# Two decode layers over a long KV cache: when a K slot is transposed, and who copies it back

## The chip, the cores and the metric

The kernel runs on one core of a Trainium2 chip. The metric is device time in microseconds, the median of several runs. A profile of one execution was taken beside it.

## The reference

Batch 8, one new token per row, model width 512, 32 query heads in 8 groups (one K/V head each, head size 128), a cache of 8192 positions, all in bf16. The same attention block, with the same weights and the same cache, and the same feed-forward block are applied twice:

```
x = A_x                                        # [8, 1, 512]
for layer in (0, 1):
    q = layernorm(x) @ wq                      # 32 heads of 128
    s = einsum(q, k_cache) * 128 ** -0.5       # k_cache [8, 8, 8192, 128]
    o = einsum(softmax(s), v_cache)            # v_cache [8, 8, 8192, 128]
    x = x + o @ wo
    x = x + silu(layernorm(x) @ w1) @ w2       # w1 [512, 1792]
```

## The kernel before

The work is cut into 128 **tasks**, one for each layer, batch row and K/V head. A task has 8 positions called **granules** (GPT = 8); a granule is 8 chunks of 128 cache rows. Two granules (GPG = 2) make a **slot**: 2048 cache rows of K or V, 512 KB, 4 KB in each of 128 partitions of an SBUF arena with NSLOT = 28 slots. So a task reads 4 slots of K and 4 of V.

Because both layers read the same cache, K of heads 3 to 7 (20 slots, KEEP) is kept in its transposed form from layer 0 to layer 1 of the same batch row. `make_tasks` orders the tasks so that it can be: after the first row come repeating groups of about 16, in which 5 layer-0 tasks with a home for their K ("home tasks") are followed by some 6 tasks of heads 0 to 2 of either layer ("streaming tasks", K and V pass through the remaining 8 slots), then by the 5 layer-1 tasks whose K lies in the arena ("kept tasks", only V is loaded). 88 tasks transpose their K, 40 don't.

One loop over positions p (from L830) emits everything; the order in which it emits is the order of each engine's queue. In a task with transposes:

- `emit_t` (L503) transposes one granule on TensorE, 8 matmuls against the identity into one of three PSUM banks TPp (L512), and copies the bank back over the raw K in the arena, on ScalarE (L518) or VectorE (L520). Three copies in eight, by the numbers in ACT_EVAC, go to ScalarE.
- `emit_t_until(p + LT)` keeps the transposes LT = 2 positions ahead of the score.
- At each odd p, `emit_s` (L537, matmuls L543) scores the slot that ends there: 4 matmuls over 512 columns each. Then `emit_pv` (L605, L616) multiplies two granules of V that lie LP = 12 positions back, 16 matmuls. I call these two positions a step.
- The softmax of the task just scored runs in pieces at set positions of the next task (the table `soft`, L817): row maximum at 0; the shift, by a small matmul (L564), and the exponential on ScalarE (L576) at 1; row sums at 3; the transposes of P (`emit_pt`, L592, in a TPp bank as well) at 4; the reciprocal at 7.
- The rest of a batch row's layer (output projection, layer norms, feed-forward, next query) is a list `chain`, of which one or two pieces are emitted per position. `add_heads` puts pieces of the output projection (L711) into kept and home tasks.

All loads go through SyncE's queue, in the order of `plan_loads` (L188). It takes the loads by their `need`, the position where they are first read, and gives each a slot by when that slot falls free (`free`), on an assumed clock of 1.24 us a position (0.64 where K is kept). A load is issued at the position `after`, when its slot's last reader is emitted; SyncE then waits for that reader. For K the need is LT positions ahead of the first granule:

```
need = -1 if i0 < PRE else i0 - LT
...
need = i0 + GPG - 1 + LP          # V
```

V loads are tried four slots wide, then two, then one: a wide one is taken only if its lead on the assumed clock is at least EARLIEST (14 us for four, 9 for two). Among free slots the planner takes the longest lead up to ENOUGH = 10 us, then the least waste, then the latest slot. Home K is loaded four slots at once, streaming K one slot at a time (KWIDE = 1).

Engines are ordered by semaphores: `op` makes an instruction wait for the last writer of what it reads and for all readers of what it overwrites. A score waits for both halves of its slot, and a copy for its transposes.

Of the kernel before, what the change touches and what calls it, by code (L numbers as in the profile page):

```python
# [14 lines left out]
GPT = 8  # L15
GPG = 2
NSLOT = 28
KEEP = 20
LT = 2
PRE = 10  # L20
KWIDE = 1
VWIDE = 4
# [1 line left out]
ENOUGH = 10.0  # L24
# [12 lines left out]
PVN = 12  # L37
CW = 32
SETTLE = 1
ACT_EVAC = (1, 4, 7)  # L40

BF16 = mybir.dt.bfloat16
FP32 = mybir.dt.float32
# [144 lines left out]
def plan_loads(tasks, kept, nslot, ngran):  # L188

    at = {t: i for i, t in enumerate(tasks)}  # L190
    homes = make_homes(kept, nslot, ngran)
    clock = [0.0]
    for layer, _b, g in tasks:
        for i in range(GPT):
            clock.append(clock[-1] + PACE[int(layer == 1 and (g, i // GPG) in kept)])
    clock += [clock[-1] + PACE[0] * (n + 1) for n in range(LP + GPT)]

    heap = []

    def push(kind, i, ks, home=None):  # L200
        layer, b, g = tasks[i]
        i0 = i * GPT + ks[0] * GPG
        if kind == "K":
            need = -1 if i0 < PRE else i0 - LT
            end = i if home is None else at[(1, b, g)]
            free = [end * GPT + (k + 1) * GPG - 1 for k in ks]
        else:
            need = i0 + GPG - 1 + LP
            free = [i * GPT + (k + 1) * GPG - 1 + LP for k in ks]
        heapq.heappush(heap, (need, kind, i, ks, Load(kind, i, b, g, ks, need, free, home)))  # L210

    def split(ks, width):
        return [ks[n:n + width] for n in range(0, len(ks), width)]

    reserved = [[] for _ in range(nslot)]
    for i, (layer, b, g) in enumerate(tasks):
        if layer == 0 and g in homes:
            ks, slot = homes[g]
            push("K", i, ks, slot)
            for n in range(len(ks)):  # L220
                reserved[slot + n].append(i * GPT + ks[0] * GPG - LT)
        for ks in split([k for k in range(ngran) if (g, k) not in kept], KWIDE):
            push("K", i, tuple(ks))
        for ks in split(list(range(ngran)), VWIDE):
            push("V", i, tuple(ks))

    def lead(need, after):
        return clock[max(0, need)] - clock[after] if after >= 0 else FAR

    free = [-2] * nslot  # L230
    loads = []
    while heap:
        d = heapq.heappop(heap)[-1]
        n = len(d.ks)
        if d.home is not None:
            for m in range(n):
                reserved[d.home + m].pop(0)
        else:
            best = None
            for slot in range(nslot - n + 1):  # L240
                held = free[slot:slot + n]
                if any(r and lead(r[0], f) < AHEAD for r, f in zip(reserved[slot:slot + n], d.free)):
                    continue
                after = max(held)
                waste = sum(clock[max(0, after)] - clock[max(0, f)] for f in held)
                key = (-min(lead(d.need, after), ENOUGH), waste, -after, slot)
                best = key if best is None else min(best, key)
            if n > 1 and (best is None or -best[0] < EARLIEST[n]):
                push(d.kind, d.task, d.ks[:n // 2])
                push(d.kind, d.task, d.ks[n // 2:])  # L250
                continue
            d.slot = best[-1]
        d.after = max(free[d.slot:d.slot + n])
        assert d.after < d.need or d.need == -1 and d.after == -2, (d.kind, d.need, d.after)
        free[d.slot:d.slot + n] = d.free
        loads.append(d)
    return loads

# [17 lines left out]
def _build(ctx, nc, A_x, A_k_cache, A_v_cache, A_wq, A_wo, B_w1, B_w2, out):  # L276
# [18 lines left out]
    NG = len(tasks) * GPT  # L295
# [20 lines left out]
    def chunk(slot, c):  # L316
        o = slot * SLOT + c * 128
        return ARENA[:, o:o + 128]
# [121 lines left out]
    with nc.Block() as block:  # L440

        @block.sync
        def _(sync_eng):
# [45 lines left out]
            load_rest()  # L489

            evacs = [0]
            tevacs = [0]
            tnext = [0]

            def has_t(i):
# [3 lines left out]
            def where(i):  # L499
                _l, b, g = tasks[i // GPT]  # L500
                return b, g, (i % GPT) // GPG, i % GPG

            def emit_t(i):  # L503
                b, g, k, h = where(i)
                slot = k_slot[(b, g, k)]
                n = tevacs[0]
                tevacs[0] += 1
                tb = evacs[0] % NTP
                evacs[0] += 1
                tpv = TPp[tb][:, :].rearrange("p (k q) -> p k q", q=128)  # L510
                steps = [
                    lambda c=c: pe.transpose(tpv[:, c, :], chunk(slot, h * GRP + c), ident[:, :])  # L512
                    for c in range(GRP)
                ]
                mm_group(steps, reads=[r_half(slot, h), "ident"], writes=[f"TP{tb}"])
                dst = half(slot, h)
                if n % 8 in ACT_EVAC:
                    op(act, lambda: act.copy(dst, TPp[tb][:, :]), reads=[f"TP{tb}"], writes=[r_half(slot, h)])  # L518
                else:
                    op(dve, lambda: dve.tensor_copy(dst, TPp[tb][:, :]), reads=[f"TP{tb}"], writes=[r_half(slot, h)])  # L520

            def emit_t_until(i):
                while tnext[0] <= min(i, NG - 1):
                    if has_t(tnext[0]):
                        emit_t(tnext[0])
                    tnext[0] += 1
# [10 lines left out]
            def emit_s(i):  # L537
                ti = i // GPT
                b, g, k, _h = where(i)
                slot = k_slot[(b, g, k)]  # L540
                bank, qn = ti % NSCP, ti % NQB
                steps = [
                    lambda c=c: pe.matmul(  # L543
                        SCp[bank][c * QUAD:(c + 1) * QUAD, :], QB[qn][:, NGRAN - 1 - k:NGRAN - 1 - k + QUAD],
                        ARENA[:, slot * SLOT + c * KB:slot * SLOT + (c + 1) * KB],
                        start=(k == 0), stop=(k == NGRAN - 1),
                    )
                    for c in range(NQ)
                ]
                mm_group(steps, reads=[r_half(slot, 0), r_half(slot, 1), f"QB{qn}"], writes=[f"SC{bank}"])  # L550
# [279 lines left out]
            for p in range(NG + LP + GPT + 1):  # L830
                tq = (p + LQ) // GPT
                if (p + LQ) % GPT == 0 and tq < ntask:
                    layer, b, _g = tasks[tq]
                    if layer == 1 and chain and chain_b[0] == b:
                        while chain:
                            chain.pop(0)()
                    emit_q(tq)
                emit_t_until(p + LT)
                if p % GPG == GPG - 1:
                    if p < NG:  # L840
                        emit_s(p)
                    for i in range(p - LP - GPG + 1, p - LP + 1):
                        if 0 <= i < NG:
                            emit_pv(i)
                ti, ph = p // GPT - 1, p % GPT
                if 0 <= ti < ntask and ph in soft:
                    for f in soft[ph]:
                        f(ti)
                if chain:
                    left = max(1, first1[chain_b[0]] - EARLY - p)  # L850
                    late = len(chain) <= QPARTS or len(chain) > left + QPARTS // 2
                    for _n in range(2 if late and len(chain) > left else 1):
                        chain.pop(0)()
                elif heads[turn[0]] and (p >= NG or turn[0] == B
                                         or p % GPG == GPG - 1 and (tasks[p // GPT][2], 0) in kept):
                    add_heads(turn[0])
                done = p - LP - GPT
                if done >= 0 and done % GPT == 0 and done // GPT < ntask:
                    tj = done // GPT
                    emit_norm(tj)  # L860
                    layer, b, _g = tasks[tj]
                    if layer == 0:
                        heads[b].append(_g)
                    elif b == B - 1:
                        heads[B].append(_g)
                    if layer == 0 and tj == last0[b]:
                        assert not chain and turn[0] == b
                        chain.extend([lambda b=b: add_heads(b)] * (HKV - summed[b]) + chain_of(b))
                        chain_b[0] = b
                        turn[0] = b + 1  # L870
                issue_until(p)
# [48 lines left out]
```

## Time and profile before

| | |
|---|---|
| median of 3 runs | 1208.91 us (1202.98 to 1213.16) |
| the profiled execution | 1205.91 us, span on the core 1204.2 us |
| busy: TensorE matmuls | 975.9 us (81%) |
| busy: VectorE | 597.2 us (50%) |
| busy: ScalarE | 374.0 us (31%) |
| bytes by DMA | 467.94 MB, mean 389 GB/s |
| mean granted TensorE clock | 0.957 |
| K loads | 192 of 512 KB, 40 of 2048 KB |
| V loads | 256 of 512 KB, 128 of 1024 KB |
| copies of transposed K | 440 on VectorE (0.690 us each), 264 on ScalarE (1.009 us each) |

Busy times are sums over an engine's instructions; a busy share says nothing by itself of what an engine waits for, and the DMA share is a mean over 16 DMA engines. PE is TensorE's matmuls, PEld its weight loads, which overlap them; a matmul's duration includes its way through the array, so the distance from start to start is what counts when the engine's pace is read.

### The profile page before, as it was taken

The page shows a single profiled execution, that of the slowest core. Times are in us where ns is not written, and L with a number is a line of the kernel's source. Part 1 is how long each engine was busy: PE and PEld are TensorE (multiplying, and loading weights), DVE is VectorE, ACT ScalarE, POOL GpSimd, SP SyncE. Part 2 cuts the span into 40 slices and gives each one's busy share as a digit, 9 for nine tenths or more (in the row PEclk, how much of TensorE's full clock was granted, in tenths as well). Part 3 has the DMA queues.
Part 4 walks back from the last instruction along what each step waited for, and adds up shares of the span by engine and source line. Part 5 has one row for each costly group of instructions (what it writes and reads, how often), then busy time and mean ns, then how long its engine had stood idle before and what let it go on. Part 6 is the DMA issues. An engine that isn't in the chain of part 4 may idle for free. (4 is left out here: it accounts for less than half of the span.)

```text
span 1204.2 us, 44647 instructions
## 1 busy us (share of the span) xinstructions
PE 975.9 (81%) x19960; PEld 766.5 (64%) x19960; DVE 597.2 (50%) x1830; ACT 374.0 (31%) x658; POOL 70.6 (6%) x172
## 2 busy tenths in 40 slices
PE   2788797888878897888878897888878887888885
PEld 2566675766656675677667675677566665767564
DVE  2345553556445553556445553556445544556444
ACT  1234331333133321443223322333133322333231
POOL 0000000000000000000000000000000000000000
PEclk9789999999999998999989998999989999999996
DMA  9999999999999999999999999999999999999994
GB/s 346 398 423 400 377 377 418 422 379 377 389 422 405 383 364 423 421 383 376 410 422 388 380 371 421 422 351 366 411 422 383 377 366 422 419 376 381 399 412 161
DMA packets 95903, 467.94 MB, mean 389 GB/s; under 512 B 9936, under 2 KB 15840, under 8 KB 73696
## 3 DMA queue, kind: packets, MB, share of 16 engines
q1 hardware_dynamic: 95712, 465.10, 97.7%
q8 instruction: 156, 2.56, 0.8%
q14 instruction: 35, 0.29, 0.1%
HBM read 465.05 MB, written 0.01 MB: 386 GB/s over the span
## 5 line engine op out<-in xcount | busy, mean ns | idle before, releaser
L520 DVE COPY arena<-TPp 128x1024 bf16<-128x1024 bf16 x440 | 303.4, 690 | 410.0 <-PE TPp L512 409.8
L512 PE MATMUL TPp<-ident,arena 128*128 128x128 bf16 x5632 | 412.7, 225 | 105.2 <-DMA arena<-in_A_k_cache_dram 88.3
L512 PEld LDWEIGHTS TPp<-ident,arena 128*128 128x128 bf16 x5632 | 342.4, 101 | 118.8 <-DMA arena<-in_A_k_cache_dram 98.3
L518 ACT COPY arena<-TPp 128x1024 bf16<-128x1024 bf16 x264 | 266.4, 1009 | 308.5 <-PE TPp L512 308.5
L616 PEld LDWEIGHTS OTp<-PT,arena 128*128 128x128 bf16 x8192 | 246.7, 97 | 169.3 <-issue 130.8
L616 PE MATMUL OTp<-PT,arena 128*128 128x48 bf16 x8192 | 301.6, 185 | 43.2 <-DMA arena<-in_A_v_cache_dram 16.8
L576 ACT ACTIVATE P<-SCp,small 128x512 bf16<-128x512 f32 x128 | 87.9, 687 | 467.7 <-DVE small L572 284.8
L543 PE MATMUL SCp<-arena,QB 128*32 128x512 bf16 x2048 | 210.7, 402 | 2.9 <-ACT QB L535 1.6
L584 POOL PARTITION_ALL_REDUCE small<-small x128 | 55.7, 435 | 947.1 <-DVE small L582 919.7
L554 DVE TENSOR_REDUCE small<-SCp 128x1 f32<-128x512 f32 x128 | 87.6, 684 | 39.9 <-PE SCp L543 39.5
L543 PEld LDWEIGHTS SCp<-arena,QB 128*32 128x32 bf16 x2048 | 53.1, 93 | 51.0 <-issue 5.1
L592 PE MATMUL TPp<-ident,P 128*128 128x128 bf16 x512 | 51.0, 223 | 33.1 <-ACT P L576 22.6
L564 PE MATMUL OTp<-P,small 128*128 128x64 f32 x256 | 54.4, 294 | 22.9 <-DVE P L556 22.2
L592 PEld LDWEIGHTS TPp<-ident,P 128*128 128x128 bf16 x512 | 30.8, 98 | 45.2 <-ACT P L576 26.6
L564 PEld LDWEIGHTS OTp<-P,small 128*128 128x128 f32 x256 | 38.3, 188 | 30.5 <-DVE P L556 28.9
L567 DVE SCALAR_TENSOR_TENSOR P<-OTp,small 128x64 f32<-128x64 f32 x128 | 36.3, 284 | 42.2 <-PE OTp L564 41.4
L582 DVE TENSOR_SCALAR small<-small 128x4 f32<-128x4 f32 x128 | 28.6, 223 | 36.7 <-ACT P L576 36.7
L596 DVE COPY PT<-TPp 128x256 bf16<-128x256 bf16 x128 | 36.9, 288 | 10.0 <-PE TPp L592 10.0
L711 PE MATMUL MISC<-at,wo 128*128 128x32 bf16 (+1 forms) x1152 | 39.8, 175 | 0.3 <-DVE at L630 0.3
L693 PE MATMUL MISC<-small,wq 128*128 128x32 bf16 x1024 | 35.0, 177 | 1.2 <-issue 1.2
L711 PEld LDWEIGHTS MISC<-at,wo 128*128 128x128 bf16 x1152 | 35.0, 96 | 0.4 <-DVE at L630 0.4
L556 DVE TENSOR_SCALAR P<-ident,small 128x64 f32<-128x64 bf16 x128 | 32.6, 254 | 4.5
(59 smaller groups left out, 300.4 us busy)
## 6 DMA issues: line engine op xcount, KB each, us to landing
arena<-in_A_v_cache_dram SPq DMA_DIRECT2D x128, 1024.0 KB, 10.4
arena<-in_A_v_cache_dram SPq DMA_DIRECT2D x256, 512.0 KB, 7.1
arena<-in_A_k_cache_dram SPq DMA_DIRECT2D x192, 512.0 KB, 7.7
arena<-in_A_k_cache_dram SPq DMA_DIRECT2D x40, 2048.0 KB, 14.7
wq<-in_A_wq_dram SPq DMA_DIRECT2D x1, 4096.0 KB, 16.8
wo<-in_A_wo_dram SPq DMA_DIRECT2D x1, 4096.0 KB, 29.6
w<-in_B_w_dram SPq DMA_DIRECT2D x2, 1792.0 KB, 25.2
P<-in_A_x_dram SPq DMA_DIRECT2D x1, 8.0 KB
```

What stands on the lines that cost most here:

```text
L512: lambda c=c: pe.transpose(tpv[:, c, :], chunk(slot, h * GRP + c), ident[:, :])
L518: op(act, lambda: act.copy(dst, TPp[tb][:, :]), reads=[f"TP{tb}"], writes=[r_half(slot, h)])
L520: op(dve, lambda: dve.tensor_copy(dst, TPp[tb][:, :]), reads=[f"TP{tb}"], writes=[r_half(slot, h)])
L543: lambda c=c: pe.matmul(SCp[bank][c * QUAD:(c + 1) * QUAD, :], QB[qn][:, NGRAN - 1 - k:NGRAN - 1 - k + QUAD], ARENA[:, slot * SLOT + c * K ...
L554: op(dve, lambda: dve.tensor_reduce(rowmax, SCp[bank][:, :], AX.X, ALU.max), reads=[f"SC{bank}"], writes=["rowmax"])
L564: mm_group([lambda: pe.matmul(every, ones.to_broadcast([128, 128]), spread, start=True, stop=True)], reads=["ones", "P"], writes=[f"OT{ob}"])
L576: op(act, lambda: act.activation(P[:, :], SCp[bank][:, :], ACT.Exp, bias=shift, scale=SM_SCALE, accum_out=rs[st]), reads=[f"SC{bank}", "sh ...
L584: op(pool, lambda: pool.partition_all_reduce(ssa[st], ssm[st], 128, bass.bass_isa.ReduceOp.add), reads=[f"ssm{st}"], writes=[f"ssa{st}"])
L592: lambda c=c: pe.transpose(tpv[:, c, :], P[:, c * 128:(c + 1) * 128], ident[:, :])
L596: op(dve, lambda: dve.tensor_copy(PT.rearrange("p x (c q) -> p x c q", q=USED), tpv.rearrange("p x (c q) -> p x c q", q=QUAD)[:, :, :, 0:U ...
L616: lambda c=c, cc=cc: pe.matmul(otp, chunk(slot, h * GRP + c), pv[:, cc % CPB, cc // CPB % NQ, k, :].unsqueeze(2).to_broadcast([128, REP, P ...
L711: lambda o=o, h=h: pe.matmul(MISC[:, o * w:(o + 1) * w], wo_sb[:, h, o * 128:(o + 1) * 128], rhs_of(h).to_broadcast([128, w]) if n == 1 el ...
```

## The change

The transposes are no longer ahead. At each odd position p the loop now emits the transposes and copies of both granules of the slot that ends at p, then two granules of PV, then the score of that slot, which waits for both copies. Half 0 of a slot is always copied by ScalarE, half 1 by VectorE. The planner's need of a K load moves from two positions before the slot's first granule to the slot's last, the reservation of home slots likewise, and among slots that are otherwise equal the planner prefers those that held V (`keys`).

```
-LT = 2
-ACT_EVAC = (1, 4, 7)
...
 def plan_loads(tasks, kept, nslot, ngran):
...
-            need = -1 if i0 < PRE else i0 - LT
+            need = -1 if i0 < PRE else i0 + GPG - 1
...
-                reserved[slot + n].append(i * GPT + ks[0] * GPG - LT)
+                reserved[slot + n].append(i * GPT + (ks[0] + 1) * GPG - 1)
...
+    keys = [0] * nslot
...
-                key = (-min(lead(d.need, after), ENOUGH), waste, -after, slot)
+                key = (-min(lead(d.need, after), ENOUGH), waste, -after, sum(keys[slot:slot + n]), slot)
...
+        keys[d.slot:d.slot + n] = [int(d.kind == "K")] * n
...
             def emit_t(i):
...
-                if n % 8 in ACT_EVAC:
+                if h == 0:
                     op(act, lambda: act.copy(dst, TPp[tb][:, :]), reads=[f"TP{tb}"], writes=[r_half(slot, h)])
                 else:
                     op(dve, lambda: dve.tensor_copy(dst, TPp[tb][:, :]), reads=[f"TP{tb}"], writes=[r_half(slot, h)])
...
-                emit_t_until(p + LT)
                 if p % GPG == GPG - 1:
-                    if p < NG:
-                        emit_s(p)
+                    emit_t_until(p)
                     for i in range(p - LP - GPG + 1, p - LP + 1):
                         if 0 <= i < NG:
                             emit_pv(i)
+                    if p < NG:
+                        emit_s(p)
```

More of the change, by code (lines that the diff above doesn't have):

```diff
@@ L491, in _ @@
             evacs = [0]
-            tevacs = [0]
             tnext = [0]
@@ L505, in emit_t @@
                 slot = k_slot[(b, g, k)]
-                n = tevacs[0]
-                tevacs[0] += 1
                 tb = evacs[0] % NTP
```

## The prediction

> **What bounds the kernel now.** The 40 slices of the page come first: the DMA row is 9 from end to end while PE stands between 7 and 8, so transfers look like the bound; but the bytes moved differ by stage, so the table by stretches of 30 us was read next.
>
> ```profile
> 60.00:90.00 30.00, 23.96 (x456) 19.42 (x453) 13.64 (x34) 9.61 (x15) 0.86 (x2) 0.89 1.01 423
> 120.00:150.00 30.00, 23.76 (x505) 19.12 (x502) 15.90 (x54) 10.34 (x17) 2.06 (x5) 1.00 0.99 377
> ```
>
> The last three columns are the granted clock, the DMA share and GB/s. At 60 us K comes in 2 MB transfers and V in 1 MB ones: 423 GB/s. At 120 us both come in 512 KB transfers, issued one by one as slots fall free: 377. A task that streams K and V needs 4.19 MB, 9.9 us at 423 and 11.1 at 377. Next, the waits:
>
> ```profile
> PEld TPp L512 <- DMA arena<-in_A_k_cache_dram: 98.3, 89, 5.4
> ...
> PEld OTp L616 <- DMA arena<-in_A_v_cache_dram: 38.4, 81, 1.7
> ```
>
> So TensorE waits for transfers for under 137 us of 1204, a good part of it at the start and where kept tasks give way to layer-0 home tasks. The rest of the time it paces itself. What it does when nothing is late is seen in the timeline of a streaming task that has its data (the first one after the home tasks):
>
> ```profile
> 792.86 0.40 PE L543 MATMUL SCp<-arena,QB 128*32 128x512 bf16 x4
> ...
> 793.19 0.57 PE L616 MATMUL OTp<-PT,arena 128*128 128x48 bf16 x16
> 793.59 0.90 PEld L512 LDWEIGHTS TPp<-ident,arena 128*128 128x128 bf16 x16
> 793.61 1.05 PE L512 MATMUL TPp<-ident,arena 128*128 128x128 bf16 x16
> ...
> 794.25 0.69 DVE L520 COPY arena<-TPp 128x1024 bf16<-128x1024 bf16 x1 [0.96 <-PE TPp L512]
> ...
> 794.59 0.40 PE L543 MATMUL SCp<-arena,QB 128*32 128x512 bf16 x4
> ...
> 795.89 0.43 PE L564 MATMUL OTp<-P,small 128*128 128x64 f32 x2 [0.39 <-DVE P L556]
> ...
> 796.16 1.06 PE L512 MATMUL TPp<-ident,arena 128*128 128x128 bf16 x16
> 796.36 0.28 DVE L567 SCALAR_TENSOR_TENSOR P<-OTp,small 128x64 f32<-128x64 f32 x1
> 796.68 0.22 DVE L572 TENSOR_REDUCE small<-P 128x1 f32<-128x64 f32 x1
> 796.99 0.69 ACT L576 ACTIVATE P<-SCp,small 128x512 bf16<-128x512 f32 x1 [3.00 <-DVE small L572]
> ...
> 797.66 1.00 ACT L518 COPY arena<-TPp 128x1024 bf16<-128x1024 bf16 x1
> ...
> 798.72 0.40 PE L592 MATMUL TPp<-ident,P 128*128 128x128 bf16 x4 [0.22 <-ACT arena L518]
> ...
> 801.23 0.40 PE L543 MATMUL SCp<-arena,QB 128*32 128x512 bf16 x4
> ```
>
> From its predecessor's last score (792.86) to its own (801.23) it takes 8.37 us. Starts on PE: PV to transposes 793.19 to 793.61, 0.42; sixteen transposes to score 0.98; score to PV (794.59 to 794.93) 0.33; so a step of two granules needs 1.73, four of them 6.92. The shift matmul (795.89 to 796.16) adds 0.27, the PT transposes about 0.24, and their two waits (for VectorE, 0.5; for a transpose bank, 0.4) make 8.3. The account closes, so the same rows can price the new order. A score here never waits for copies: its granules were transposed a step earlier.
>
> **The tasks, by kind.** Distances between the scores that end consecutive tasks: the first task ends at 37.4 us, then 40 home tasks (layer 0, heads 3 to 7) 387 us (9.7 each), 40 kept tasks (layer 1, same heads, no K load and no transposes) 256 (6.4), 47 streaming ones 501 (two at the start, held by the weights, 30; the other 45 10.5 each), and 22 after the last score: 1204.
>
> **The change, part by part.**
>
> Transposes, PV, score in one step. Counted from the first transpose: PE is through sixteen transposes at 0.89 (weight loads, 0.90) and through PV's sixteen matmuls at 0.89 + 0.57 = 1.46. The copy of half 0 on ScalarE starts at 0.64 (793.61 to 794.25) and takes 1.00: 1.64. Half 1's transposes end 0.45 later, so VectorE starts at 1.09 and takes 0.69: 1.78. A matmul released by VectorE starts 0.06 after it (L556 ends 795.83, L564 starts 795.89): the score starts at 1.84, and the next step's transposes at 1.84 + 0.33 = **2.17** against 1.73. PV covers only part of the copies; some 0.4 us of every step is a wait on PE, with all of the later PE stream queued behind it.
>
> The copies' split, one half on each engine, takes VectorE from 440 copies to 352 and ScalarE from 264 to 352. Neither total binds (597 and 374 us busy). But order binds: at the second position of a task the exponential (L576) is queued on ScalarE ahead of the next step's half-0 copy. From the shift matmul to that engine being free takes 797.66 - 795.89 = 1.77 us; the next transposes start 0.27 after the shift, so the copy runs from 1.50 to 2.51 of its step and the score starts at 2.57, not 1.84: 0.73 once a task. Before, a copy had a step to spare. VectorE's row maximum and spread (0.68 + 0.25) fit between a half-1 copy and the next (done about 1.0 after the step starts): nothing. The two old waits go: the maximum no longer stands before the shift with copies between, and no transpose bank is still in use when PT needs one.
>
> A task with transposes therefore has a floor of 4 x 2.17 + 0.27 + 0.24 + 0.73 = **9.92 us, up from 8.37**.
>
> The block chains (8 of them, between a layer-0 and a layer-1 pass of a batch row): their 240 matmuls cost some 6 us of PE before and after (28 take 0.70 start to start, 16 take 0.40). Their layer norms now stand before copies that a score waits for: third and fourth stage are 13 VectorE operations at about 0.2, some 1.1 us beyond the room left in a step, twice a chain, plus a few tenths at the activation: 2.5 us a chain, bounds 0 and 5.
>
> Planner. K is needed at its own step, three positions later, and slots fall free where they did: two at each odd position, in eight streaming slots. K had 7 positions from release to need and V 6 (VectorE and PE rows do not show this; it is the planner's arithmetic); now each has 8. V does not become wider: a pair needs 9.0 us, 8 positions of 1.24, in two adjacent slots, and K takes one of the two slots free that early; the other pairs with one at 6 positions, 7.4 us. So the number of transfers and the SP issues (0.33 to 0.47 us each, one per transfer) stay. With the new tie rule K takes the slot that held V, which PV frees before the score: no cost on SP's queue, where K now leads. The gain is depth: 16 positions of lead instead of 13, which the 377 GB/s stretches want. Its bounds are nothing and the whole of TensorE's waits for transfers in tasks with transposes, 53 + 25 us streaming and 27 home by the gaps, of which some 25 belong to the start: 0 to about 80.
>
> **The sum.** Streaming: 45 tasks at 10.1 (between the floor 9.92 and 10.3, 4.19 MB at 408 GB/s, what full stretches of 512 KB transfers reach) plus 8 chains at 8.5: 522, against 471: +51. Home: the floor and 0.3 for output-projection pieces is 10.2, transfers at 422 need 9.9; coupled 10.3: 412 against 387, +25. Kept: their first two tasks take 5.9 now against 4.9 later in the stage for want of V; deeper leads take 1 off each, 8 times: -16; the wait for the first home K (about 5 us a group) stays, as transfers run at 422 there. Start and tail: nothing. Total +60; from the other side, 85 floors at +1.55 and 8 chains at +2.5 give +152, less 80 of waits absorbed and 16: +56. I take +56: span 1260. The profiled run took 1205.91 for a span of 1204.20, and the three runs' median is 1208.91; I forecast **1262** on the run's own scale.
>
> A rule of the Trainium skill speaks against the new order. The rows first: in stretches where PE stopped for 0.5 to 1.1 us in most steps (120 to 200 us) the granted clock stayed 1.00; it fell mainly where PE had stopped for 2 us and more (0.59 in the stretch 205 to 210 us, with a wait of 3.6). The Trainium skill's "TensorE: Matmul & The Clock Gate", section "A second HAM failure mode: psum-queue depth-cycling", says that short idles between matmul groups can by themselves make the clock swing between half and full. The trace goes against that here; by the rule the time would be that of the last rival below.
>
> **Rivals.**
> 1. *Depth wins* (faster). For: the 377 GB/s stretches, 45 tasks at 10.5 where 9.9 would do. Against: it needs the score's wait to cost nothing, thus VectorE's copy ready by 1.46, while 1.78 follows from two rows. It decides once a task's floor is below some 9.6 us. Then streaming falls to 455, kept by 16: 1172.
> 2. *A draw.* The exponential does not stand in front of the copy (ScalarE reaches it earlier than its order says): 0.73 x 88 = 64 less: 1198.
> 3. *Waits on top.* Lead in time hardly grows and half of the 90 us of DMA waits remain beside the new floor: 1262 + 45 = 1307. Against: slower steps ask less of the queues.
> 4. *Half clock in every step.* Eight transposes then take 0.82 instead of 0.45 (both spacings occur in the trace), the second copy starts near 1.9, the step takes 3.2: 352 x 1.0 more, above 1600.
>
> **How the numbers follow.** Forecast 0.73, rivals 0.10, 0.09, 0.06, 0.02. The range takes in the draw below and most of rival 3 above: 1196 to 1300, leaving out depth, half of rival 3 and rival 4, 0.15. The forecast's own range is 1230 to 1290: a tenth of a microsecond in the step is 35 us, and chain and depth have the bounds above. About 1% is what a measurement of this kernel can tell from no change: faster 0.10, same 0.09, slower 0.81.
>
> **What would show it.** Right: score matmuls (L543 now) waiting for VectorE's copies about 350 times, 0.3 to 0.5 us each, longer once a task for ScalarE's; waits of transposes for K nearly gone; streaming and home tasks at 10 us or more; DMA share below 0.97; transfer counts the same. Wrong: a score that starts at PV's end, tasks under 9.6 us, stretches at 405 GB/s or more throughout, or V transfers of 1 MB in the streaming stages.

## The result, and the profile after

The changed kernel takes 1291.94 us (median of 4 runs, 1290.53 to 1294.51), the kernel before 1211.04 in the same comparison: a ratio of 1.0683, 95% interval 1.0629 to 1.0738. The profiled execution took 1292.0 us for a span of 1290.3.

The same two stretches of 30 us, with granted clock, DMA share and GB/s in the last three columns, now read:

```profile
60.00:90.00 30.00, 23.26 (x450) 19.51 (x451) 12.31 (x31) 12.30 (x19) 1.01 (x3) 0.94 0.99 401
120.00:150.00 30.00, 22.15 (x434) 18.81 (x435) 15.42 (x53) 13.14 (x20) 2.12 (x5) 0.98 0.96 360
```

Both move fewer bytes than before (423 and 377 GB/s), and the share of the DMA queue over the span fell, though the bytes are the same. Packets, MB and share, before and after:

```profile
q1 hardware_dynamic: 95712, 465.10, 97.7%
...
q1 hardware_dynamic: 92256, 465.10, 94.2%
```

Transfers are no longer what is late. In the list of waits (total us, times, longest) the ones for data, 38 us for V and 98 for K before, have shrunk to this; all but 2 us of K's are at the start:

```profile
PEld OTp L613 <- DMA arena<-in_A_v_cache_dram: 14.7, 18, 1.9
...
PEld TPp L509 <- DMA arena<-in_A_k_cache_dram: 9.6, 5, 7.7
```

and a new one stands in their place, the score matmuls (L540 now) behind the copies. In the page's costliest groups the last column is TensorE's idle time just before them. The row before the change and after it:

```profile
L543 PE MATMUL SCp<-arena,QB 128*32 128x512 bf16 x2048 | 210.7, 402 | 2.9 <-ACT QB L535 1.6
...
L540 PE MATMUL SCp<-arena,QB 128*32 128x512 bf16 x2048 | 216.3, 411 | 207.6 <-DVE arena L517 68.3
```

Of these 208 us the page ascribes only 68 to VectorE's copy; in other steps it names whatever VectorE or ScalarE instruction ran last, as the timeline shows. Here is a home task in which no transfer costs anything (one of V is 0.3 us late for the PV at 400.63, but the score behind it starts 1.94 after its transposes, as elsewhere); its predecessor's last score is the one at 398.89, its own the one at 409.45:

```profile
396.96 1.05 PE L509 MATMUL TPp<-ident,arena 128*128 128x128 bf16 x16
397.60 1.01 ACT L515 COPY arena<-TPp 128x1024 bf16<-128x1024 bf16 x1 [1.56 <-PE TPp L509]
...
397.85 0.56 PE L613 MATMUL OTp<-PT,arena 128*128 128x48 bf16 x16
398.05 0.69 DVE L517 COPY arena<-TPp 128x1024 bf16<-128x1024 bf16 x1 [1.98 <-PE TPp L509]
...
398.89 0.40 PE L540 MATMUL SCp<-arena,QB 128*32 128x512 bf16 x4 [0.48 <-DVE small L600]
...
399.22 1.07 PE L509 MATMUL TPp<-ident,arena 128*128 128x128 bf16 x16
...
401.76 1.06 PE L509 MATMUL TPp<-ident,arena 128*128 128x128 bf16 x16
...
402.54 0.69 ACT L573 ACTIVATE P<-SCp,small 128x512 bf16<-128x512 f32 x1 [1.65 <-DVE small L569]
...
403.22 1.00 ACT L515 COPY arena<-TPp 128x1024 bf16<-128x1024 bf16 x1
...
404.27 0.40 PE L540 MATMUL SCp<-arena,QB 128*32 128x512 bf16 x4 [1.05 <-ACT arena L515]
...
409.45 0.40 PE L540 MATMUL SCp<-arena,QB 128*32 128x512 bf16 x4 [0.47 <-DVE small L600]
```

A step runs from transposes at 396.96 to transposes at 399.22: 2.26 us. PV has ended at 398.41 and VectorE's copy at 398.74, the score starts at 398.89. Behind the exponential (402.54) ScalarE's copy ends at 404.22 and the score starts at 404.27, 2.51 after its transposes. This task takes 10.56 us with one projection piece of 0.40; tasks without such a piece take 10.16 at the least, where the old floor was 8.37.

Distances between the scores that end consecutive tasks, summed by kind as in the prediction (us):

| | first task | 47 streaming | 40 home | 40 kept | after the last score | span |
|---|---|---|---|---|---|---|
| before | 37.4 | 501 | 387 | 256 | 22.5 | 1204.2 |
| foreseen | 37.4 | 552 | 412 | 240 | 22 | 1260 |
| after | 33.9 | 565 | 425 | 244 | 21.9 | 1290.3 |

The row "foreseen" adds up to 1263 by the task kinds; the forecast had taken 1260.

### The profile page after: what moved, and what is told of

The parts are those of the page before. It is cut to its first block, busy times and chain, and to the rows that moved or that the text cites. A ratio compares the mean times of both kernels' runs of the same rounds, so it can differ in the third digit from the quotient of the medians.

```text
span 1290.3 us, 45003 instructions
## 1 busy us (share of the span) xinstructions
PE 967.9 (75%) x19960; PEld 786.5 (61%) x19960; DVE 564.4 (44%) x1742; ACT 462.5 (36%) x746; POOL 70.6 (5%) x172
## 5 line engine op out<-in xcount | busy, mean ns | idle before, releaser
L515 ACT COPY arena<-TPp 128x1024 bf16<-128x1024 bf16 x352 | 355.4, 1010 | 419.0 <-PE TPp L509 418.9
L509 PE MATMUL TPp<-ident,arena 128*128 128x128 bf16 x5632 | 384.9, 223 | 20.7 <-DVE arena L517 10.3
L540 PE MATMUL SCp<-arena,QB 128*32 128x512 bf16 x2048 | 216.3, 411 | 207.6 <-DVE arena L517 68.3
L509 PEld LDWEIGHTS TPp<-ident,arena 128*128 128x128 bf16 x5632 | 336.7, 100 | 46.6 <-issue 37.0
L517 DVE COPY arena<-TPp 128x1024 bf16<-128x1024 bf16 x352 | 243.2, 691 | 272.2 <-PE TPp L509 271.3
L613 PEld LDWEIGHTS OTp<-PT,arena 128*128 128x128 bf16 x8192 | 268.1, 98 | 67.1 <-issue 52.0
L540 PEld LDWEIGHTS SCp<-arena,QB 128*32 128x32 bf16 x2048 | 61.4, 94 | 245.4 <-ACT arena L515 170.7
L708 PEld LDWEIGHTS MISC<-at,wo 128*128 128x128 bf16 x1152 | 34.0, 97 | 13.5 <-issue 13.1
L690 PEld LDWEIGHTS MISC<-small,wq 128*128 128x128 bf16 x1024 | 29.5, 96 | 7.9 <-issue 7.9
## 6 DMA issues: line engine op xcount, KB each, us to landing
arena<-in_A_k_cache_dram SPq DMA_DIRECT2D x40, 2048.0 KB, 13.1
```

The source lines that it names most:

```text
L540: lambda c=c: pe.matmul(SCp[bank][c * QUAD:(c + 1) * QUAD, :], QB[qn][:, NGRAN - 1 - k:NGRAN - 1 - k + QUAD], ARENA[:, slot * SLOT + c * K ...
L613: lambda c=c, cc=cc: pe.matmul(otp, chunk(slot, h * GRP + c), pv[:, cc % CPB, cc // CPB % NQ, k, :].unsqueeze(2).to_broadcast([128, REP, P ...
L708: lambda o=o, h=h: pe.matmul(MISC[:, o * w:(o + 1) * w], wo_sb[:, h, o * 128:(o + 1) * 128], rhs_of(h).to_broadcast([128, w]) if n == 1 el ...
```

## The experiments

The theory: a step's score waits in TensorE's queue for two copies beside which there is too little work, and this, not the split, the planner or PV's place, is the loss. Rivals: the split of the copies; the new plan of loads; PV in front of the score; and transfers that would hold the time anyway. Ratios are to the kernel before.

### The split alone

```
 (before)      if n % 8 in ACT_EVAC:   ->   if h == 0:
```

> The kernel before with one edit: half 0 of every slot is copied by ScalarE, half 1 by VectorE; the order and the planner stay. Theory (the score waits for copies beside too little work, in the new order): here a score follows its copies by a whole step, so the split costs nothing: 1200 to 1220 us, tasks with transposes that have their data at about 8.4 us. Rival (the split itself, 88 more copies of 1.01 us on ScalarE, some behind the exponential, is what costs): 1240 us or more.

Measured: 1199.89 us, ratio 0.9914 (0.9898 to 0.9931). The split by itself makes the old kernel a little faster: its floor for a task with transposes falls from 8.4 to 7.8 us, the sums by kind hardly move (500, 386, 254), and TensorE only waits longer for K, 117 us for 98 in the list of waits. The rival is out.

### The old split in the new order

```
 (after)       if h == 0:   ->   if i % 8 in (1, 4, 7):
```

> The kernel after with the old split of copies (the second, fifth and eighth granule of a task on ScalarE, the rest on VectorE). Theory: what counts is when the later of a slot's two copies ends. Vector then Scalar: 1.09 + 1.01 = 2.10, score near 2.15; two on VectorE: 0.64 + 0.69 + 0.69 = 2.02 and 0.15 to the score, 2.17; Scalar then Vector 1.93 as now. A task has two, one and one of these, and the step behind the exponential has both copies on VectorE, so 2.17 for 2.51 there. Per task 0.22 + 0.22 - 0.34 = +0.1 us: 1285 to 1315 us. Rival (the split is at fault): 1240 or less.

Measured: 1312.82 us, ratio 1.0851 (1.0822 to 1.0880). The total is as the theory had it. In the steps two of the three sizes were off: a score starts 2.26 after its first transpose where VectorE copies first and ScalarE second (foreseen 2.15), 1.99 where VectorE copies both (foreseen 2.17), and 1.93 in the third kind, as foreseen. Within the new order the split by halves is the better one.

### The score without its wait

```
-   ARENA[:, slot * SLOT + c * KB:slot * SLOT + (c + 1) * KB],
+   wq_sb[:, c, 0:KB],
...
-   reads=[r_half(slot, 0), r_half(slot, 1), f"QB{qn}"]
+   reads=["wq", f"QB{qn}"]
```

> The kernel after, but the score multiplies a resident weight and does not read the K slot, so that it waits for no copy; transposes, copies, loads and their slots are all still there, and only the scores are not those of K. Theory: the step falls from 2.26 us to about 1.75, the exponential's 0.58 once a task goes too, and the transfers become the bound, with leads of 8 positions: 1160 to 1200 us. Rival (depth does not help, transfers ran at 375 GB/s for want of something else): about 1210. Rival (the wait for copies is not what costs): above 1250.

Measured: 1194.10 us, ratio 0.9869 (0.9837 to 0.9902). Without the wait 98 us go, more than the change had added. Tasks with transposes that have their data take 8.0 us. So the wait is what the change costs. The edit takes one more thing away, which the expectation did not name: a K slot's next load no longer waits for the score to have read it. But the kernel then stands only 6 us below the one with the split alone, whose leads are shorter, and waits for V again:

```profile
PEld OTp L613 <- DMA arena<-in_A_v_cache_dram: 72.1, 83, 3.0
...
PEld TPp L509 <- DMA arena<-in_A_k_cache_dram: 35.7, 61, 7.5
```

The streaming stretch of 120 to 150 us moves 397 GB/s here for 377 before. What the deeper leads are worth in time is not separated by this: the two kernels differ in their order too, and their intervals overlap.

### Work moved into the wait

The score is emitted behind the softmax, chain and projection pieces of its position:

```
                     for i in range(p - LP - GPG + 1, p - LP + 1): ... emit_pv(i)
-                    if p < NG:
-                        emit_s(p)
                 ...  # soft pieces, chain, add_heads
+                if p % GPG == GPG - 1 and p < NG:
+                    emit_s(p)
```

> The kernel after with the score emitted behind the softmax pieces, chain pieces and output projection pieces of its position, so that these run on TensorE while the copies end. Theory: the shift matmul (0.27), the output projection pieces (0.40) and about half of the chain pieces fall into the wait of 0.5 us, and the exponential starts 0.8 us earlier against the next copy, which takes away its delay of 0.58: a home task goes from 10.6 to 9.3 by TensorE and is then held by transfers at 9.9; streaming tasks lose 1 us: 1205 to 1245 us. Rival (PE's waits are set by transfers, not by order): 1280 to 1300, no change.

Measured: 1226.47 us, ratio 1.0160 (1.0098 to 1.0223). 65 us come back from the same instructions in another order. The floor of a task is 9.32 us, home tasks sum to 410 and streaming ones to 519, and ScalarE's copy is the later one in 35 steps, at 2.08 instead of 2.51.

### The copy behind the exponential

```
 (after)       if h == 0:   ->   if h == 0 and i % GPT != GPG:
```

> The kernel after with one copy moved: at the step behind the exponential (third granule of a task) half 0 is copied by VectorE, too. Theory: the score there starts 2.51 us after the step's first transpose because ScalarE is held by the exponential; with two copies on VectorE it starts at 0.64 + 0.69 + 0.69 + 0.15 = 2.17, 0.34 less, in the 61 to 88 steps where ScalarE is last now: 21 to 30 us less, 1260 to 1275. Rival (the exponential's delay is hidden by other waits, or VectorE's queue gives it back): 1285 or more.

Measured: 1270.55 us, ratio 1.0496 (1.0441 to 1.0550): 21 us less than after. The floor falls by 0.52, from 10.16 to 9.64, not by 0.34: the two copies on VectorE take less together than two of them apart, and the score follows them sooner.

```profile
402.92 1.06 PE L509 MATMUL TPp<-ident,arena 128*128 128x128 bf16 x16
403.58 1.28 DVE L517 COPY arena<-TPp 128x1024 bf16<-128x1024 bf16 x2
...
404.91 0.40 PE L540 MATMUL SCp<-arena,QB 128*32 128x512 bf16 x4 [0.53 <-DVE arena L517]
```

Two copies in 1.28 us, where one takes 0.69; they end at 404.86 and the score starts 0.05 later.

### The plan of loads

```
-   need = -1 if i0 < PRE else i0 + GPG - 1
+   need = -1 if i0 < PRE else i0 - 2
...  # the reservation likewise, and no keys
```

> The kernel after with the planner of before (K needed two positions ahead of its slot, no preference for slots that held V), so K's lead is 7 positions and V's 6 instead of 8 and 8. Theory (TensorE sets the pace, so depth is worth nothing here): 1280 to 1305 us. Rival (the deeper leads already pay in the new order and hide a larger loss): 1315 or more. Rival (the new plan costs something): 1275 or less.

Measured: 1288.77 us, ratio 1.0639 (1.0591 to 1.0687), against 1.0683 (1.0629 to 1.0738): no difference that these intervals can tell. In this order neither a gain from the leads of 8 positions nor a cost of the new plan can be seen.

### Score first where there are no transposes

```
+                    first = p < NG and not has_t(p)
+                    if first: emit_s(p)
                     emit_t_until(p)
                     ...  # PV
-                    if p < NG:
+                    if p < NG and not first:
                         emit_s(p)
```

> The kernel after, but where a slot needs no transposes (kept tasks) its score comes before PV, as it did. Theory: in a kept task the chain from the last score over maximum, shift and exponential to the transposes of P sets the pace, and PV ahead of the score makes it about 0.5 us longer: kept tasks fall from 5.6 at the least to 4.9, and in sum by 10 to 25 us, some of it given back as a wait for the next home K: 1265 to 1285 us. Rival (kept tasks are held by transfers): 1290 as after.

Measured: 1277.89 us, ratio 1.0539 (1.0497 to 1.0581). Kept tasks sum to 201 us instead of 244 (foreseen were 10 to 25 less, it is 43), and the shortest goes from 5.61 to 4.77. Home tasks sum to 452 instead of 425: the first of each group takes 12.6 to 16.1 us, as it then waits for its K,

```profile
PEld TPp L509 <- DMA arena<-in_A_k_cache_dram: 22.8, 9, 6.7
```

23 us in this list for 9.6 after. So PV ahead of the score does lengthen kept tasks, by way of the softmax, and two thirds of that is covered by a transfer that is late anyway. The same edit on top of the work moved into the wait:

> The kernel that scores behind the softmax, chain and projection pieces (1226 us), and scores first where a slot needs no transposes. Theory: TensorE still sets the pace of streaming tasks there, and kept tasks fall from 5.6 to 4.9; since transfers are nearer to their limit, at most half of it shows: 1208 to 1226 us. Rival (transfers give all of it back): 1226 as without.

Measured: 1213.46 us, ratio 1.0023 (0.9999 to 1.0047): 13 us of the 35 that kept tasks lose show.

### Which copy the score waits for last

By then the timelines gave one number for nearly every step: the score starts 0.146 us after the later copy's end if that is half 1's (273 of 287 steps), and 0.053 if it is half 0's (all 61). In the program the wait for half 0 comes first. The two were exchanged:

```
-   reads=[r_half(slot, 0), r_half(slot, 1), f"QB{qn}"]
+   reads=[r_half(slot, 1), r_half(slot, 0), f"QB{qn}"]
```

> The kernel after with the two waits of a score exchanged: it waits for half 1's copy (VectorE) first and for half 0's (ScalarE) second. In the runs so far a score starts 0.146 us after the end of the later copy where that copy is the one it waits for second, on either engine, and 0.053 us where it is waited for first or both copies are on one engine. Theory (the second wait of an instruction costs 0.09 more): in the 287 steps where VectorE is last the score starts 1.84 instead of 1.93 after the step's first transpose, in the 61 where ScalarE is last 0.09 later than now: about 20 us less, 1268 to 1276 us. Rival (a copy of this size is released late): no change, 1288 to 1294.

Measured: 1280.78 us, ratio 1.0557 (1.0499 to 1.0615), a profiled span 16 us shorter than after's, the medians 11 apart. The steps did what the theory said:

```profile
397.33 1.00 ACT L515 COPY arena<-TPp 128x1024 bf16<-128x1024 bf16 x1
398.48 0.40 PE L540 MATMUL SCp<-arena,QB 128*32 128x512 bf16 x4 [1.02 <-ACT arena L515]
399.04 1.06 PE L509 MATMUL TPp<-ident,arena 128*128 128x128 bf16 x16
...
400.14 0.69 DVE L517 COPY arena<-TPp 128x1024 bf16<-128x1024 bf16 x1 [0.53 <-PE TPp L509]
400.88 0.40 PE L540 MATMUL SCp<-arena,QB 128*32 128x512 bf16 x4 [0.38 <-DVE arena L517]
```

After ScalarE's copy (ends 398.33), now the second wait, 0.15; after VectorE's (ends 400.83) 0.05, and the score 1.84 after its transposes. It is the place of the wait, not the engine or the size of the copy. The total came out a little above the 1268 to 1276 foreseen (the four runs lie between 1276 and 1286); where the rest went was not followed.

### PV first, transposes ahead

The kernel with the split alone, and `emit_pv` before `emit_s`:

> The kernel before with the split by halves (1200 us) and with PV ahead of the score, the transposes still two positions ahead. Theory: the score waits for nothing new, tasks with transposes keep their floor near 7.8 to 8.2 us; kept tasks go from 4.9 at the least to 5.6, and the wait for the first home K takes that up: 1195 to 1210 us. Rival (PV ahead of the score is what costs in the change): 1230 or more.

Measured: 1209.44 us, ratio 0.9972 (0.9934 to 1.0010). The sums by kind are 499, 384 and 256. PV's place alone is not what the change costs; against the split alone (0.9914) it may cost some 0.6%.

### The best of the new order

Score behind the pieces, score first in kept tasks, waits exchanged:

> The kernel that scores behind the softmax, chain and projection pieces, scores first where there are no transposes (1213 us), and waits for half 1's copy first. Theory: 0.09 less in each of some 320 steps is 29 us of TensorE's time, of which transfers, now near their limit, give back half or more: 1193 to 1207 us. Rival (transfers give all back): 1213.

Measured: 1200.97 us, ratio 0.9914 (0.9878 to 0.9950). This version beats the kernel before by a little under 1%, and the old order with the new split (0.9914) does so with one edited line. They cannot be told apart by time.

## Why the prediction was right, and where its sizes were off

**What bounds the kernel.** 1292 lies within the range of 1196 to 1300, but 2 us above the forecast's own 1230 to 1290, and the loss is 81 us where 53 were foreseen. The mechanism is right: the loss is TensorE's own order, shown by taking the wait away (1194) and by filling it (1226) with the same loads in place.

**The step, 2.17 us, was 0.09 short.** It came out at 2.26. Every term held but one: the copies start and end at 0.64, 1.65, 1.09 and 1.78 as worked out, and the score follows 0.146 later, not 0.06. The 0.06 was taken from an instruction that had one wait to pass; a score has two, on two engines, and the late one is the second. Over the 348 steps that wait (the first task transposes before the loop) 0.09 is 31 us, and 30 lie between the forecast's span of 1260 and 1290. That the two agree is partly luck: the exponential, next, was priced too high and gives back 9 to 13 of them, and chains and kept tasks add what is missing. The exchange of the waits shows the term at its size in the steps.

**The exponential, 0.73, was 0.58.** Its score starts at 2.51 for 2.57 foreseen, and the ordinary step against which it counts at 1.93. Moving that copy to VectorE brought 21 us. Floor of a task: 9.92 foreseen, 10.16 measured.

**Chains, 8.5 us each, came out at some 9.4.** The four tasks that a chain spans sum to 48.0 to 52.3 us in the eight groups; less four floors of 10.16 that is 7.4 to 11.7. What makes the longer ones long was not followed.

**Home tasks, 10.3, came out at 10.6,** the floor's error again, and 0.4 for a projection piece instead of 0.3. Behind the first of each group (10.4 to 13.1) they are so even, 10.2 without a piece and 10.6 with one, that hardly anything but TensorE's order is left in them.

**Kept tasks: the right sum for the wrong reason.** 244 against 240. Foreseen was a gain of 16 from deeper leads, with the 5 us wait for the first home K unchanged. In fact that wait went, because home K had time to land, and each task got about 0.7 longer at the least, because PV now delays its score and the softmax behind it. That cost was not in the sum at all. Nor was the clock, which makes some kept tasks longer still (below): 40 at the shortest, 5.61, would be 224. Projection pieces of 0.40 and the clock are most of the other 20.

**Depth.** Leads of 8 positions are what the plan gives for most streaming loads. That they are worth 0 to 80 us was too generous above: in the new order nothing that shows (the old plan), and with the wait out of the way 6 us against the split alone and 15 against the kernel that also has PV first, which differ from it in more than depth. So the first rival, 1172, would not have come even if the score had waited for nothing. That the number of transfers stays was wrong: 24 more V pairs of 1 MB are loaded (152 for 128, most of them in kept tasks), without effect that shows. Of the rivals, the draw needed ScalarE to take the copy out of order, and it did not.

**The rule on the clock.** In the steps it did not bite. Home tasks stop for the score by 0.47 us in most steps, by 1.05 behind the exponential, and from 390 to 420 us the granted clock stays 1.00. Stages of kept tasks are another matter. The first of these two stretches has home tasks, the second mostly kept ones (granted clock third from the right):

```profile
390.00:420.00 30.00, 22.71 (x467) 19.03 (x464) 13.21 (x34) 13.76 (x21) 1.29 (x3) 1.00 0.97 388
...
1200.00:1230.00 30.00, 23.85 (x424) 15.87 (x425) 10.02 (x36) 4.77 (x15) 1.72 (x4) 0.79 0.99 370
```

From 346.8 to 363.8 us, and from 1206.9 to 1237.6, the granted clock is 0.5 and 1.0 by turns, in stretches of 3.4 us, though TensorE's longest stop there is 0.77 us. A kept task has two stops close together, 0.76 for the exponential and 0.47 for VectorE (L627); in the full-clock stretches between, TensorE is busy for 2.0 to 2.3 of 3.4 us, in home tasks (395 to 420 us) for 77% of the time. Kept tasks without a projection piece take 5.6 us where the clock stays full, as from 782 to 793 us with the same stops, and 6.4 to 6.5 with 3 us at half clock. So what the prediction read in the old trace, that the clock falls mainly behind stops of 2 us and more, does not hold for the kept tasks of the new one. The mean hides this: it is 0.956 for 0.957. The Trainium skill's "TensorE: Matmul & The Clock Gate", section "A second HAM failure mode: psum-queue depth-cycling", would let short idles swing the clock between half and full. This trace shows such a swing in kept tasks, not in the steps where the last rival had put it.

## What to carry to other kernels

Before a lookahead is removed to save buffer time, count what an in-order engine has to do between giving work away and needing it back: here 0.5 us of PV stood against the 1.0 us from the end of the transposes' issue to the score, 348 times, and depth that was no longer needed could not pay for it. If the wait has to be there, emit the independent pieces of the same position into it, and order waits so that the one that comes last is passed first. Price a release by a row with the same number of waits, not by the nearest short one.

## What the runs showed of the hardware

A score matmul that waits on two engines starts 0.053 us after the later copy's end if it waits for that copy first, and 0.146 if second, on either engine. Two VectorE copies of 128x1024 in a row take 1.28 us, not twice 0.69. The granted clock changed between 0.5 and 1.0 every 3.4 us in stretches of kept tasks whose longest stop was 0.77 us, and stayed 1.00 in home tasks (390 to 420 us) with a stop of 0.47 us in most steps and 1.05 once a task. And with every slot refilled 8 positions ahead and no wait for the copies, 30 us stretches of 512 KB transfers ran at 358 to 409 GB/s (366 to 379 before), where home tasks with 1 and 2 MB transfers ran at 400 to 424; what still holds the slower of them was not tried.
